# A hand-written order of the first eight steps, changed: conversions on GpSimd moved beside VectorE's rows, one product split around a weight folding, weight differences and sums moved, loads of x earlier

## The chip, the core and the metric

The kernel runs on one core of a Trainium2 chip. The metric is the device time of one execution in microseconds (us), from a median of several runs. The core has TensorE (PE, the matrix engine; PEld is its loading of weights), VectorE (DVE), ScalarE (ACT), GpSimd (POOL) and the queue of SyncE (SP), from which nearly all transfers (DMAs) are issued. Each engine works through its own list of instructions in order and waits for the others by semaphores. Matrix products write to PSUM, which here has eight banks; the rest lives in SBUF.

## The reference

An FFT over the sequence and one over the features, of which the real part is kept, and behind it a two-layer network with the quick Gelu:

```python
X = np.fft.fft(x, axis=1)          # x: (8, 3008, 256) float32
X = np.fft.fft(X, axis=2)
x = X.real.astype(np.float32).reshape(24064, 256)
h = x @ w_in                        # w_in: (256, 2048), 64-bit floats
g = h * (1.0 / (1.0 + np.exp(-1.702 * h)))
out = (g @ w_out).astype(np.float32)   # w_out: (2048, 256), 64-bit floats
```

## The kernel before, in words

**The two transforms.** The sequence of 3008 is taken as 47 times 64. For each of the eight batches `fold1` adds and subtracts mirrored rows and columns of x in SBUF (on GpSimd), `mix1` does the transform over 47 (TensorE), `spill` and `fill` turn the result through DRAM (`Td`), `rotate` corrects one column, `stage2` does the transform over 64, and `nyquist` spreads one special row. The transform over the 256 features is not done on x: `fold_w(n)` multiplies it into `w_in` once, chunk by chunk (n = 0 to 3, 512 columns each), and the result stands in `wcs[0]` (cosines) and `wcs[1]` (sines). Since x is real, rows k and -k of the hidden layer are sum and difference of the same two products.

**The weights.** `w_in` and `w_out` come as 64-bit floats and are made 32-bit on the chip, in eight chunks ("in" 0 to 3, "out" 0 to 3). For each chunk: `sizes` takes the absolute value of the upper word (L450 on ScalarE or L452 on VectorE), `clamp` bounds it (L456, GpSimd), `low` takes the lower word (L460, ScalarE), `high` shifts and masks (L486 and L487, VectorE), and `finish` adds both (L499 `finish_in`, L507 `finish_out`, GpSimd). `bounds(key)` calls sizes, clamp and low. `third` treats chunk "in" 2 in two halves of 512. `halved(n)` (L512, L513, VectorE) makes a sum and a difference of the finished chunk, which `fold_w(n)` (L533, copies L540 on ScalarE) multiplies; its copies of the result are needed by `hidden` and `first_row(n)`. `differences(n)` (L525, four subtractions on GpSimd) and `small_weights(n, lo, hi)` (L751, up to four sums on VectorE) prepare `w_out` for products in the manner of Strassen and Winograd: seven products for eight, and a second such level below.

**The steps.** The hidden layer is worked in 384 steps t: 8 batches, 3 blocks, 2 halves, 8 pairs of 128 columns each. The first eight (t = 0 to 7, the first group) run with plain products: `hidden(t)` makes the two sums pa and pb in two PSUM banks and copies pa to v (L584, ScalarE); `rows(t)` (VectorE: L614, two of L619, L621) makes both hidden rows; `activate(t)` (L625) is the Gelu; `product(t, lo, hi)` multiplies with `w_out` (a plan of eight entries; `lo` and `hi` cut it). `first_row(n)` (bank psf; copies L548 and L549) gives rows(2n), rows(2n + 1) and later steps a scale. From t = 8 on, a step is `begin` (x, in the bank `b0` or `b1`, on which ScalarE's `middle`, L634, has laid a start value), `forward` (L649), `doubled` (L646), `backward` (L653), `activate_back` (L656), `sums` (L664 and L665 on GpSimd; L671 and L672 on VectorE at odd t, in step t + 1), `deeper` (L695, L697, L699) and, three steps later, `product` with its `small_products` (L740).

**The order.** What each engine does next follows from the order in which the program is written out. For t < 8 that is `hidden(t)` and then the list `SCRIPT[t]`; at t = 7 `middle(8)` comes before `hidden(7)` and `begin(8)` right behind it. `extra` holds what is done at the end of a step t, entered by `at(t, ...)`; entries of one step run in the order in which they were entered. PLANS gives, for batch 0 and for the others, the steps of the sixteen folds, of the four `mix1`, the first `fill`, the `rotate`, the four loads of x for the batch after next (`load_x`, into the one buffer `xt`) and the three `stage2`. `paced(t)` issues a transfer of 4 bytes that waits for `forward(t)`, so that SP does not run ahead. Banks not named are taken in turn from `spare`; from step 5 on these are `o2`, `o3`, `o4` and `b2`: folding 3 takes o2 and o3, hidden(6) o4 (pa) and b2, first_row(3) o2, hidden(7) o3 (pa) and o4 (pb).

Of the kernel before, what the change touches and what calls it, by code (L numbers as in the profile page):

```python
# [121 lines left out]
def kernel(ctx: ExitStack, tc, x, w_in, w_out, tab1, tab2, out):  # L122
# [331 lines left out]
    def clamp(key, lo=0, n=1024):  # L454
        g = pre[key][0][:, lo:lo + n]
        nc.gpsimd.tensor_scalar(g, g, scalar1=TOP, scalar2=LOW, op0=ALU.min, op1=ALU.max)  # L456
# [5 lines left out]
    def third():  # L462

        prepare(in2)
        for h0 in (0, 512):
            sizes(in2, nc.vector, h0, 512)
            clamp(in2, h0, 512)
        low(in2)
        for h0 in (0, 512):
            high(in2, h0, 512)  # L470
            finish_in(2, h0, 512)

    def bounds(key):
        prepare(key)
        sizes(key, nc.scalar)
        clamp(key)
        low(key)

    def high(key, lo=0, n=1024):

        bits = pre[key][0][:, lo:lo + n].bitcast(U32)
        if lo == 0:
            made_a[key] = ring("a").bitcast(U32)
        a = made_a[key][:, lo:lo + n]
        dve = nc.vector
        dve.tensor_scalar(a, bits, scalar1=3, scalar2=0x3FFFFFF8, op0=ALU.logical_shift_left, op1=ALU.bitwise_and)  # L486
        dve.scalar_tensor_tensor(a, raw[key][:, lo:lo + n, 1], 0xC0000000, a, op0=ALU.bitwise_and, op1=ALU.bitwise_or)  # L487
# [5 lines left out]
    def finish_in(n, lo=0, k=1024):  # L493

        if lo == 0:
            wst[n] = op.tile([128, 2, 512], F32, tag="os", name="wst")
        key, part = ("in", n), slice(lo, lo + k)
        out = wst[n][:].rearrange("p i f -> p (i f)")[:, part]
        nc.gpsimd.tensor_tensor(out.bitcast(U32), made_a[key][:, part], pre[key][1][:, part], op=ALU.add)  # L499
# [158 lines left out]
    def sums(t, eng):  # L658

        if not NP <= t < len(steps):  # L660
            return
        n = width(t)
        if eng is nc.gpsimd:
            eng.tensor_tensor(right(t, S1, n), left(t, A21, n), right(t, A22, n), op=ALU.add)  # L664
            eng.tensor_tensor(left(t, S3, n), left(t, A11, n), left(t, A21, n), op=ALU.subtract)  # L665
            return
        if t % 2 == 0:
            return
        a11, s2 = (free(big[:], at_left(t - 1, q), [1024, 2], [1, n]) for q in (A11, S2))
        a12, s4, s1 = (free(big[:], at_right(t - 1, q), [1024, 2], [1, n]) for q in (A12, S4, S1))  # L670
        eng.tensor_tensor(s2, s1, a11, op=ALU.subtract)  # L671
        eng.tensor_tensor(s4, a12, s2, op=ALU.subtract)  # L672
# [69 lines left out]
    def small_weights(n, lo=0, hi=4):  # L742

        def y(i, at):
            return free(wot[:], (2 * n + i) * 4 * H + 2 * H + at, [NF // 2 * 4 * H, 2], [H, 2], [1, 64])

        b11, b12, b21, b22 = y(0, 0), y(0, 64), y(1, 0), y(1, 64)
        t1, t2, t3, t4 = (free(big[:], MADE + n * 1024 + q * 128, [512, 2], [64, 2], [1, 64]) for q in range(4))
        for out, i0, i1, how in ((t1, b12, b11, ALU.subtract), (t2, b22, t1, ALU.add), (t3, b22, b12, ALU.add),
                                 (t4, b21, t2, ALU.subtract))[lo:hi]:  # L750
            nc.vector.tensor_tensor(out, i0, i1, op=how)  # L751
# [218 lines left out]
    for h0 in (0, 512):  # L970
# [10 lines left out]
    halved(1)  # L981

    extra = {}
    PLANS = (((*range(9, 18), 22, 23, 24, 25, 26, 29, 30), (20, 28, 28, 36), 38, 43, (41, 42, 43, 44), (8, 20, 44)),
             ([g + k for g in (0, 8, 16, 24) for k in range(-2, 2)], (4, 20, 28, 28), 31, 35, (36, 38, 40, 42), (4, 20, 36)))

    def at(t, fn, *args):
        extra.setdefault(t, []).append((fn, args))
# [8 lines left out]
    if B > 1:  # L997
# [4 lines left out]
        at(6, nc.vector.memset, both_ends[0:1, 1, :], 0.0)  # L1002
        at(6, load_ends, 1)
        at(18, fold_ends, 1, nc.gpsimd)
    for i, t in enumerate((4, 5, 6, 7)):
        at(t, differences, i)
    for i, t in (1, 7), (2, 9):
        at(t, small_weights, i)
    for q, t in enumerate((11, 13, 14, 15)):
        at(t, small_weights, 3, q, q + 1)  # L1010
    for b in range(B):
        t0 = b * NBLK * NF
        if b + 2 < B:
# [24 lines left out]
        for blk in range(NBLK):  # L1038
# [7 lines left out]
    SCRIPT = (  # L1046
        [(nyquist, 0, 0), (fold_w, 1, ("o0", "o1")), (prepare, out0), (rows, 0, ((sizes, out0, nc.vector), (clamp, out0))), (high, out0)],
        [(low, out0), (finish, out0), (load_in, 3, nc.sync), (fill, 0, 4, NG), (activate, 0), (rows, 1)],
        [(first_row, 1), (activate, 1), (third,), (rows, 2), (halved, 2)],
        [(product, 0, 0, None), (product, 1, 0, None), (bounds, out1), (bounds, in3), (activate, 2), (high, out1), (finish, out1), (rows, 3),  # L1050
         (fold_w, 2), (activate, 3), (high, in3), (finish, in3)],
        [(first_row, 2), (rotate, 0, 4, NG, nc.scalar.copy), (rows, 4), (halved, 3)],
        [(product, 2, 0, None), (activate, 4), (bounds, out2), (rows, 5), (fold_w, 3), (activate, 5), (high, out2), (finish, out2)],
        [(first_row, 3), (product, 3, 0, None), (bounds, out3), (rows, 6), (activate, 6), (small_weights, 0), (high, out3), (finish, out3)],
        [(product, 4, 0, None), (rows, 7)])
    for t in range(n + LAG):
        if t < NP:
            if t == NP - 3:
                spare[:] = [tag for tag in spare if tag[0] == "o"] + ["b2"]
            if t == NP - 1:  # L1060
                middle(NP)
            hidden(t)
            if t == NP - 1:
                begin(NP)
                no_row(1024)
            for fn, *args in SCRIPT[t]:
                fn(*args)
            if t == NP - 1:
                doubled(NP)
                middle(NP + 1)  # L1070
        else:
            after, special = (any(fn in (mix1, stage2) for fn, _ in extra.get(k, ())) for k in (t - 1, t))
            assert t == NP or not special or (t - LAG) % NP == 1
            if t < n:
                begin(t, 1)
            if t == NP:
                activate(t - 1)
            if t < n:
                forward(t)
            if after:  # L1080
                swap(t - LAG - 3)
            opening = (t - LAG) % NP == 0 and t >= NP + LAG
            one, other = (1, 2, 4, 7), (5, 6, 3)
            cut = 0 if opening else 2
            if opening:
                small_products(t - LAG - 1, other[:2])
            else:
                product(t - LAG, 0, cut)
            if t + 1 < n:
                begin(t + 1)  # L1090
            if not after:
                small_products(t - LAG - 1, other[2 * opening:])
            if t > NP:
                spare[:] = ["l0", "l1", "l2", "b2"] if special else ["b2"]
                for fn, args in extra.get(t, ()):
                    if fn in (mix1, stage2):
                        fn(*args)
            product(t - LAG, cut, 6 if t - LAG == last else None)
            if after:
                small_products(t - LAG - 1, (7, *other, 1, 2, 4))  # L1100
            elif not special:
                small_products(t - LAG, one)
            if not special:
                swap(t - LAG - 2)
            if t < n:
                backward(t)
            if t + 1 < n:
                doubled(t + 1)
            if t < n:
                activate_back(t)  # L1110
                sums(t, nc.gpsimd)
            if t + 2 < n:
                middle(t + 2)
            for args in waiting:
                mixed(*args)
            waiting.clear()
            combine_small(t - LAG - 1)
            if t - LAG == last:
                product(last, 6, None)
            sums(t - 1, nc.vector)  # L1120
            turn_seconds()
            deeper(t - 2, 0)
            deeper(t - 3, 1)
        if t == NP:
            psu.close()
            low = ctx.enter_context(tc.tile_pool(name="low", bufs=1, space=PS))
            pot["low"] = low.tile([128, 3 * 512], F32, tag="low", name="low")
        if t >= LAG:
            combine(t - LAG)
            combine_last(t - LAG - 3)  # L1130
            turn_last(t - LAG - 4, 0)
            turn_last(t - LAG - 5, 1)
        if t == NP:
            spare[:] = ["l0", "l1", "l2", "b2"]
        for fn, args in extra.get(t, ()):
            if t <= NP or fn not in (mix1, stage2):
                fn(*args)
        if t == NP:
            turn_seconds()
# [28 lines left out]
```

## Time and profile before

| | |
|---|---|
| median of 3 runs | 1838.31 us (1837.73 to 1838.72) |
| the profiled execution | 1836.29 us, its span 1834.5 us |
| mean granted TensorE clock | 0.999 |
| busy share of the span | PE 99%, PEld 77%, DVE 81%, ACT 62%, POOL 54% |
| TensorE busy | 1819.8 us |
| DMA moved | 105.68 MB, mean 58 GB/s |
| steps 0 to 7 on TensorE | from 33.3 us to about 76.7 us of the span |

The profile is of one execution. Its parts and views give, for each engine, line of the kernel, operation and tile: when an instruction ran and how long (start, us), and after what wait ("idle before", with what ended it). In a view of waits, the columns are the line that waited, the line that ended the wait, the total, how often, and the longest. The same line number can serve many callers: L196 is the helper `halves`, through which most matmuls go, so the tile tells them apart (pa and pb: hidden; psf: first_row; psw: fold_w; o: product; x: begin). A matmul's end is modelled; the start of the next one says more.

### The profile page before, as it was taken

The page shows a single profiled execution, that of the slowest core. Times are in us where ns is not written, and L with a number is a line of the kernel's source. Part 1 is how long each engine was busy: PE and PEld are TensorE (multiplying, and loading weights), DVE is VectorE, ACT ScalarE, POOL GpSimd, SP SyncE. Part 2 cuts the span into 40 slices and gives each one's busy share as a digit, 9 for nine tenths or more (in the row PEclk, how much of TensorE's full clock was granted, in tenths as well). Part 3 has the DMA queues.
Part 4 walks back from the last instruction along what each step waited for, and adds up shares of the span by engine and source line. Part 5 has one row for each costly group of instructions (what it writes and reads, how often), then busy time and mean ns, then how long its engine had stood idle before and what let it go on. Part 6 is the DMA issues. An engine that isn't in the chain of part 4 may idle for free.

```text
span 1834.5 us, 55862 instructions
## 1 busy us (share of the span) xinstructions
PE 1819.8 (99%) x23656; PEld 1403.5 (77%) x23656; DVE 1481.7 (81%) x1927; ACT 1138.9 (62%) x2238; POOL 992.1 (54%) x1070
## 2 busy tenths in 40 slices
PE   8999999999999999999999999999999999999998
PEld 5677788777777777877778777787777877777775
DVE  7988878877888778887888878888788887878874
ACT  4556656666666656666665666666666666656663
POOL 3785556554656546565456644676446653444442
PEclk9999999999999999999999999999999999999999
DMA  9711151114210251212402124021331012100011
GB/s 283 185 53 35 43 115 28 47 36 101 54 53 23 52 117 21 62 36 67 89 22 59 32 67 86 22 64 27 87 66 39 14 27 64 30 19 14 18 24 24
DMA packets 151687, 105.68 MB, mean 58 GB/s; under 512 B 106212, under 2 KB 133094, under 8 KB 150878
## 3 DMA queue, kind: packets, MB, share of 16 engines
q1 hardware_dynamic: 148270, 99.09, 22.3%
q8 instruction: 186, 3.05, 0.7%
q10 hardware_dynamic: 3168, 3.03, 0.6%
q14 instruction: 63, 0.52, 0.1%
HBM read 64.81 MB, written 48.05 MB: 62 GB/s over the span
## 4 chain that ended last, share of the span: by engine, by line
PE 96%; DMA 2%; DVE 1%; issue 0%; POOL 0%; ACT 0%; SPq 0%; DVEq 0%; ACTq 0%; POOLq 0%
PE x L196 34%; PE o L196 27%; PE low L740 26%; PE o L740 4%; PE low L273 1%; PE low L393 1%; DMA xt<-in_x_dram 1%; PE po L196 0%; DMA big<-in_moe_w_in_dram 0%; DMA Td<-big 0%; DVE big L671 0%; DMA Td<-e 0%; DMA Tf<-big 0%; PE psw L533 0%; PE ps L393 0%
## 5 line engine op out<-in xcount | busy, mean ns | idle before, releaser
L664 POOL TENSOR_TENSOR big<-big 128x256 f32<-128x256 f32 (+1 forms) x376 | 366.4, 974 | 785.4 <-ACT big L656 764.5
L196 PE MATMUL x<-pq,wcs 128*64 128x256 f32 (+1 forms) x6016 | 767.7, 375 | 0.0
L196 PE MATMUL o<-big,wo 128*64 128x256 f32 (+1 forms) x4800 | 633.9, 376 | 1.0 <-DVE big L671 1.0
L196 PEld LDWEIGHTS x<-pq,wcs 128*64 128x64 f32 x6016 | 426.1, 137 | 170.9 <-issue 0.8
L196 PEld LDWEIGHTS o<-big,wo 128*64 128x64 f32 x4800 | 340.1, 137 | 144.9 <-issue 7.7
L646 ACT ACTIVATE g<-x 128x512 f32<-128x512 f32 (+1 forms) x376 | 221.7, 590 | 363.0 <-PE x L196 361.9
L665 POOL TENSOR_TENSOR big<-big 128x256 f32<-128x256 f32 (+1 forms) x376 | 381.3, 1014 | 0.0
L740 PE MATMUL low<-big 128*64 128x128 f32 (+1 forms) x5888 | 379.1, 270 | 0.0
L649 ACT ACTIVATE big<-x 128x512 f32<-128x512 f32 (+1 forms) x376 | 221.7, 589 | 233.9 <-PE x L196 207.7
L634 ACT ACTIVATE x<-nb,af 128x256 f32<-128x256 f32 (+1 forms) x752 | 352.7, 469 | 12.2
L653 DVE TENSOR_TENSOR big<-g,x 128x512 f32<-128x512 f32 (+1 forms) x376 | 250.5, 666 | 130.4 <-ACT big L649 129.9
L740 PEld LDWEIGHTS low<-big 128*64 128x64 f32 x5888 | 336.7, 137 | 24.9 <-DVE pq L403 0.2
L695 DVE TENSOR_TENSOR big<-big 128x1024 f32<-128x1024 f32 (+1 forms) x184 | 223.5, 1215 | 101.0 <-PE low L740 85.3
L656 ACT ACTIVATE big<-big 128x512 f32<-128x512 f32 (+1 forms) x376 | 231.6, 616 | 29.1 <-DVE big L653 28.0
L740 PE MATMUL low<-big,wo 128*64 128x128 f32 (+1 forms) x2944 | 221.8, 270 | 0.0
L699 DVE TENSOR_TENSOR big<-big 128x512 f32<-128x512 f32 (+1 forms) x184 | 191.7, 1042 | 0.0
L697 DVE TENSOR_TENSOR big<-big 128x512 f32<-128x512 f32 (+1 forms) x184 | 168.5, 916 | 16.6 <-PE o L196 0.9
L740 PEld LDWEIGHTS low<-big,wo 128*64 128x64 f32 x2944 | 174.0, 137 | 6.7 <-DVE big L699 0.5
L672 DVE TENSOR_TENSOR big<-big 128x512 f32<-128x512 f32 (+1 forms) x188 | 159.8, 850 | 6.5
L842 DVE TENSOR_TENSOR big<-big,low 128x512 f32<-128x512 f32 (+3 forms) x184 | 109.1, 610 | 35.1 <-PE low L740 31.6
L671 DVE TENSOR_TENSOR big<-big 128x512 f32<-128x512 f32 (+1 forms) x188 | 135.7, 722 | 0.9 <-POOL big L664 0.9
L740 PE MATMUL o<-big,wo 128*64 128x128 f32 (+1 forms) x1472 | 110.8, 270 | 0.0
(119 smaller groups left out, 1124.0 us busy)
## 6 DMA issues: line engine op xcount, KB each, us to landing
out_dram<-os SPq DMA_DIRECT2D x284, 64.0 KB
Td<-xt SPq DMA_DIRECT2D x56, 192.0 KB
t<-Td SPq DMA_DIRECT2D x21, 512.0 KB
xt<-in_x_dram SPq DMA_DIRECT2D x14, 512.0 KB
xt<-Xr SPq DMA_DIRECT2D x14, 512.0 KB
nb<-Nd SPq DMA_DIRECT2D x22, 256.0 KB
out_dram<-os SPq DMA_DIRECT2D x96, 56.0 KB
Xr<-in_x_dram SPq DMA_DIRECT2D x7, 752.0 KB
```

What stands on the lines that cost most here:

```text
L196: nc.tensor.matmul(out[c0:c0 + 64], lhsT=lhs[:, c0:c0 + 64], rhs=rhs, skip_group_check=True, **how)
L634: nc.scalar.activation(x[:, i * 256:i * 256 + n], nbt[b, blk][:, hh * 256:hh * 256 + n], ACTF.Copy, scale=af1[:, f:f + 1])
L646: nc.scalar.activation(two(g[:], n), two(xb[t][:], n), ACTF.Copy, scale=2.0)
L649: nc.scalar.activation(front(t), two(xb[t][:], width(t)), ACTF.Gelu_apprx_sigmoid)
L653: nc.vector.tensor_tensor(back(t), two(gt.pop(t)[:], n), two(xb.pop(t)[:], n), op=ALU.subtract)
L656: nc.scalar.activation(back(t), back(t), ACTF.Gelu_apprx_sigmoid)
L664: eng.tensor_tensor(right(t, S1, n), left(t, A21, n), right(t, A22, n), op=ALU.add)
L665: eng.tensor_tensor(left(t, S3, n), left(t, A11, n), left(t, A21, n), op=ALU.subtract)
L695: nc.vector.tensor_tensor(free(big[:], SUM, *both_), free(big[:], from11 + w, *twice), free(big[:], from11, [at_right(t, 0) + w - from11, ...
L697: nc.vector.tensor_tensor(s2, a11, s1, op=ALU.subtract)
L699: nc.vector.tensor_tensor(s4, a12, s2, op=ALU.subtract)
L740: nc.tensor.matmul(o, lhsT=lhs, rhs=rhs, start=first_in, stop=(p == NP - 2), skip_group_check=True)
```

## The change

Six things are moved; no arithmetic is changed.

1. In `third`, the second half of `finish_in(2)` is no longer called; step 2 calls it later, behind `bounds(out1)`, which moves from step 3 to step 2.
2. `bounds` can leave out its clamp. In step 3 the clamp of "in" 3 comes behind `finish(out1)`; `high` and `finish` of "in" 3 move from the end of step 3 to the end of step 4, behind `rows(4)`, and `halved(3)` from step 4 to step 5, behind `rows(5)`.
3. Product 3 moves from step 6 to step 5, half of its plan ahead of `fold_w(3)`, half behind it and `activate(5)`.
4. The four `differences` run at the ends of steps 5 to 8 and not 4 to 7. `small_weights(0)` moves from step 6 to the end of step 7, `small_weights(1)` from 7 to 8; the four parts of `small_weights(3)` run in steps 11, 13, 15 and 17, in the middle of the step behind GpSimd's `sums`, and not at the ends of 11, 13, 14 and 15.
5. Batch 1's folds: the first eight run one step later (10 to 17), the ninth at 21 and not 17; the other seven stay.
6. For batch 1, `fill` starts at step 37 and not 38 (`rotate` stays at 43), and the loads of x for batch 2 are issued at steps 39 to 42 and not 41 to 44.

```diff
--- before.py
+++ after.py
@@ -466,14 +466,15 @@
             sizes(in2, nc.vector, h0, 512)
             clamp(in2, h0, 512)
         low(in2)
-        for h0 in (0, 512):
-            high(in2, h0, 512)
-            finish_in(2, h0, 512)
-
-    def bounds(key):
+        high(in2, 0, 512)
+        finish_in(2, 0, 512)
+        high(in2, 512, 512)
+
+    def bounds(key, now=True):
         prepare(key)
         sizes(key, nc.scalar)
-        clamp(key)
+        if now:
+            clamp(key)
         low(key)
 
     def high(key, lo=0, n=1024):
@@ -981,7 +982,7 @@
     halved(1)
 
     extra = {}
-    PLANS = (((*range(9, 18), 22, 23, 24, 25, 26, 29, 30), (20, 28, 28, 36), 38, 43, (41, 42, 43, 44), (8, 20, 44)),
+    PLANS = (((*range(10, 18), 21, 22, 23, 24, 25, 26, 29, 30), (20, 28, 28, 36), 37, 43, (39, 40, 41, 42), (8, 20, 44)),
              ([g + k for g in (0, 8, 16, 24) for k in range(-2, 2)], (4, 20, 28, 28), 31, 35, (36, 38, 40, 42), (4, 20, 36)))
 
     def at(t, fn, *args):
@@ -1002,12 +1003,11 @@
         at(6, nc.vector.memset, both_ends[0:1, 1, :], 0.0)
         at(6, load_ends, 1)
         at(18, fold_ends, 1, nc.gpsimd)
-    for i, t in enumerate((4, 5, 6, 7)):
+    for i, t in enumerate((5, 6, 7, 8)):
         at(t, differences, i)
-    for i, t in (1, 7), (2, 9):
+    for i, t in (0, 7), (1, 8), (2, 9):
         at(t, small_weights, i)
-    for q, t in enumerate((11, 13, 14, 15)):
-        at(t, small_weights, 3, q, q + 1)
+    amid = {11 + 2 * q: (3, q, q + 1) for q in range(4)}
     for b in range(B):
         t0 = b * NBLK * NF
         if b + 2 < B:
@@ -1046,12 +1046,13 @@
     SCRIPT = (
         [(nyquist, 0, 0), (fold_w, 1, ("o0", "o1")), (prepare, out0), (rows, 0, ((sizes, out0, nc.vector), (clamp, out0))), (high, out0)],
         [(low, out0), (finish, out0), (load_in, 3, nc.sync), (fill, 0, 4, NG), (activate, 0), (rows, 1)],
-        [(first_row, 1), (activate, 1), (third,), (rows, 2), (halved, 2)],
-        [(product, 0, 0, None), (product, 1, 0, None), (bounds, out1), (bounds, in3), (activate, 2), (high, out1), (finish, out1), (rows, 3),
-         (fold_w, 2), (activate, 3), (high, in3), (finish, in3)],
-        [(first_row, 2), (rotate, 0, 4, NG, nc.scalar.copy), (rows, 4), (halved, 3)],
-        [(product, 2, 0, None), (activate, 4), (bounds, out2), (rows, 5), (fold_w, 3), (activate, 5), (high, out2), (finish, out2)],
-        [(first_row, 3), (product, 3, 0, None), (bounds, out3), (rows, 6), (activate, 6), (small_weights, 0), (high, out3), (finish, out3)],
+        [(first_row, 1), (activate, 1), (third,), (bounds, out1), (finish_in, 2, 512, 512), (rows, 2), (halved, 2)],
+        [(product, 0, 0, None), (product, 1, 0, None), (bounds, in3, False), (activate, 2), (high, out1), (finish, out1), (clamp, in3),
+         (rows, 3), (fold_w, 2), (activate, 3)],
+        [(first_row, 2), (rotate, 0, 4, NG, nc.scalar.copy), (rows, 4), (high, in3), (finish, in3)],
+        [(product, 2, 0, None), (activate, 4), (bounds, out2), (product, 3, 0, 4), (rows, 5), (halved, 3), (fold_w, 3), (activate, 5),
+         (product, 3, 4, None), (high, out2), (finish, out2)],
+        [(first_row, 3), (bounds, out3), (rows, 6), (activate, 6), (high, out3), (finish, out3)],
         [(product, 4, 0, None), (rows, 7)])
     for t in range(n + LAG):
         if t < NP:
@@ -1109,6 +1110,8 @@
             if t < n:
                 activate_back(t)
                 sums(t, nc.gpsimd)
+            if t in amid:
+                small_weights(*amid[t])
             if t + 2 < n:
                 middle(t + 2)
             for args in waiting:
```

## The prediction, made before the result was known

> **What bounds the kernel now.** I read the page's first part, then the waits of TensorE, then the order of time on TensorE and its neighbours in the first group. TensorE is busy almost throughout, at a granted clock of 0.999:
>
> ```profile
> PE 1819.8 (99%) x23656; PEld 1403.5 (77%) x23656; DVE 1481.7 (81%) x1927; ACT 1138.9 (62%) x2238; POOL 992.1 (54%) x1070
> ```
>
> So the change can only win what TensorE stands still. The waits of TensorE after the opening (line that waited, who ended it, total us, times, longest):
>
> ```profile
> PE o L196 <- DVE big L671: 1.0, 2, 0.8
> ...
> PE low L393 <- issue: 0.7, 1, 0.7
> ...
> PE psf L196 <- DVE big L621: 0.4, 1, 0.4
> PE psw L533 <- DVE big L512: 0.3, 1, 0.3
> PE psw L533 <- DVE big L513: 0.3, 1, 0.3
> ```
>
> These are too small, since a matmul's end is modelled. The order of time on TensorE (start, length) gives the rest:
>
> ```profile
> 50.78 1.04 PE L533 MATMUL psw<-big,small 128*64 128x512 f32 x2 [0.32 <-DVE big L512]
> 52.13 1.93 PE L533 MATMUL psw<-big,small 128*64 128x512 f32 x6 [0.31 <-DVE big L513]
> 53.88 1.08 PE L196 MATMUL pa<-pq,wcs 128*64 128x256 f32 x8
> ...
> 66.81 0.58 PE L196 MATMUL psf<-twos,wcs 128*64 128x1 f32 x16
> 67.24 3.65 PE L196 MATMUL o<-big,wo 128*64 128x256 f32 x32
> 70.72 1.03 PE L196 MATMUL pa<-pq,wcs 128*64 128x256 f32 x8
> 71.59 1.03 PE L196 MATMUL pb<-pq,wcs 128*64 128x256 f32 x8
> 72.45 0.93 PE L196 MATMUL x<-pq,wcs 128*64 128x226 f32 x8
> ```
>
> Starts that follow each other without a wait give TensorE's prices: a pa or pb 0.87, a product 3.47, first_row 0.44, the eight records of a folding 1.73 (35.92 to 37.64). The folding of chunk 2 should begin when the products end (43.35 + 6.94 = 50.29) and take 1.73, but step 4 starts at 53.88: 1.86 us stand still. For chunk 3, from 61.99 to 65.03, it is 1.31. ScalarE behind first_row(3), in the order of time:
>
> ```profile
> 67.56 1.21 ACT L450 ACTIVATE big<-big 128x1024 f32<-128x1024 f32 x1
> 68.64 1.20 ACT L460 ACTIVATE big<-big 128x1024 uint32<-128x1024 uint32 x1
> 69.71 1.09 ACT L625 ACTIVATE big<-big 128x1024 f32<-128x1024 f32 x1
> 70.67 0.95 ACT L634 ACTIVATE x<-nb,af 128x226 f32<-128x226 f32 x2
> ```
>
> The reader is to see that this row of four ends at 71.62, 4.37 us after first_row(3) ended (67.25), and that begin(8) (the x of 72.45) needs its last member; product 3 and hidden(7) cover it. VectorE against GpSimd, around 99 us:
>
> ```profile
> 99.17 2.70 DVE L671 TENSOR_TENSOR big<-big 128x452 f32<-128x452 f32 x1
> ```
> ```profile
> 98.85 1.27 POOL L247 TENSOR_TENSOR xt<-xt 111x510 f32<-111x510 f32 x1
> 100.09 0.67 POOL L664 TENSOR_TENSOR big<-big 128x226 f32<-128x226 f32 x1
> 100.71 0.66 POOL L665 TENSOR_TENSOR big<-big 128x226 f32<-128x226 f32 x1
> ```
>
> L671 takes 0.72 on average, and here it ends some 0.5 us after three GpSimd instructions in a row. VectorE's rows (L614 to L621, which read PSUM) keep 0.69, 0.86 and 0.69 beside L507 at 54 us. That is what "beside the rows" can use.
>
> **The change part by part.** All sums are against the profiled execution's 1836.29 us (span 1834.5 and 1.8 around it); the median of the runs shown is 1838.31, 2.0 above it.
>
> *Step 2 and the folding of chunk 2.* GpSimd gets the clamp of out1 (L456, 1.04) between the two halves of finish_in(2). The second half, 47.80 to 49.08 before, waits for VectorE's L487 (47.73) and then for the clamp: it ends near 49.9. It lies beside rows(2), which ends at 49.83. So halved(2) starts 0.2 later, but its second half no longer meets the clamp of in3 (L513 took 1.52 beside L456; alone 0.68), and ends at 51.2 and not 52.08. ScalarE's two conversions of out1 (1.1 each) now stand ahead of the copy v(3), which nobody needs before 53. Step 4 begins 1.75 after L513 (as 52.13 to 53.88): at 53.0, a gain of 0.88. Bounds: nothing (if the clamp gets ahead of L487) and 0.9.
>
> *Steps 3 to 5 and the folding of chunk 3.* high(in3), 1.9 us on VectorE, filled the time between rows(3) and rows(4). Now rows(4) follows rows(3) at once: that ends at 55.2, then activate(3) (1.06) and the copy v(4) (0.58) must pass on ScalarE before rows(4) can start at 56.9. VectorE idles 1.6. Then rows(4) 2.2, high(in3) 1.9 to 60.9, finish_in(3) on GpSimd (L499, 2.36) to 63.3 beside rows(5). halved(3) comes behind rows(5), and behind the clamp of out2, which is next on GpSimd and ready (1.04): its halves end near 64.9 and 65.5, not 62.09 and 63.23. TensorE, 0.84 earlier at hidden(5) (its first_row(2) still waits for rows(3)), does product 2 and half of product 3 by 62.9, waits, folds from 65.0 to 66.85, and covers ScalarE's copies with the other half: it stands still 2.24 where it was 1.31, a loss of 0.93. Bounds: a gain of 1.31 (halving in time) and a loss of 1.97 (one more GpSimd instruction of 1.04 in front).
>
> *Step 6.* Product 3 has left the place between first_row(3) and hidden(7). Behind first_row(3) ScalarE still owes the 4.37 us shown, and TensorE has only hidden(7), 1.73, to lay over it. So begin(8) starts 2.7 late; before, the cover was 5.2 and nothing was lost. Also pb(7) takes the bank of pa(6) (six banks in turn) and waits for rows(6), inside the same gap. Bounds: 2.6, and 3.2 if rows(6) holds activate(6) back. Product 4 starts 0.93 + 2.7 - 0.88 = 2.75 later than 73.22.
>
> *Differences and weight sums.* The differences (four of 0.8 to 0.95 on GpSimd) come a step later; the first products that need them run 30 us on. small_weights(0) and (1) move to the ends of steps 7 and 8 (3.4 us each beside GpSimd); VectorE then gives L653 of step 8 at about 82, as before. Differences(3) now stand between sums(8) and sums(9), so forward(10) comes near 93 instead of 88.95; begin(12), on a TensorE 2.75 late, wants its result near 96.4 and gets it: nothing, covered by 0.8 us; without that cover it costs what it is late. The last sums go into VectorE's pauses: at step 11 L695 waited 0.65 for ScalarE, and L751 (0.89) now fills that instead of standing before L671. L671 then ends 0.8 earlier, and the folding beside it is another half. TensorE stands from 100.92 to 101.92 and from 110.24 to 110.59 for it: a gain of 1.35; bounds 0 and 1.35.
>
> *Folds of x, fills, loads.* The folds go a step later, the ninth from 17 to 21; GpSimd waited 764 us for L656 over the run, and the groups that use them keep their steps: nothing. On SP the first fill now follows the last spill in the same step and waits for its landing; the store behind it was waiting for VectorE until 224.37 anyway. Loads 39 and 40 queue behind the stores that end at 231.8, so data starts near 232.6 instead of 234.0. rotate stays at 43, some 12 us after its last fill. TensorE's 0.68 of "issue" in stage2 at 249 falls where the DMA share is 1.0 (234 to 256); it would be 1.0 to about 254 still: I take nothing; bounds a gain and a loss of 0.7. The Trainium skill (DMA: Bandwidth & Descriptors, Queues, rings and completion order) says that an engine takes turns between queues packet by packet; by that the fetch is as slow as long as anything is queued, the same sum. No run here shows the packets.
>
> Sum: -0.88 + 0.93 + 2.7 - 1.35 = +1.4, so 1837.7 in the profile's terms and 1839.7 as a median. Bounds added: -0.9 - 1.3 + 2.6 - 1.35 - 0.7 = -1.65 and 0 + 1.97 + 3.2 + 0 + 0.7 = +5.9.
>
> **The rivals.** *Halving in time:* chunk 3's wait goes as its products are laid around it. For it: 1.73 of TensorE's work before and 1.73 behind. Against it: 1.6 us idle before rows(4) and the clamp. It gives 1.4 - 2.24 = -0.8: 1837.5.
>
> *VectorE locked out (the slower side).* In L671's 2.70 VectorE did not get in between GpSimd's instructions; in L512 against L525 (1.21 at 60.88) it did. If it does not where GpSimd is now queued tightly, L487 waits for the clamp of out1 (no 0.88), the sums bring no 1.35, and halved(3) waits once more (1.04): 1.4 + 3.3 = +4.7, 1843.0. It decides from 2.3 us on top of my sum. The Trainium skill (SBUF — State Buffer, Who interferes with whom) says that who issues first has the shared pair for one whole instruction; by it VectorE gets in after each, and the sum stays +1.4. The 2.70 beside three does not fit that, so I keep both.
>
> *The change does all it says:* ScalarE's chain is hidden too. Then 0.88 + 1.31 + 1.35 + 0.68 = 4.2 are won: 1834.1. Against it stand the 4.37 us over 1.73.
>
> **How the numbers follow.** 0.2% (3.7 us) is about what a measurement of this kernel can tell from no change. Forecast 0.47, halving in time 0.18, locked out 0.30, all it says 0.05. Faster is the last, 0.05; within 0.2% the first two, 0.65; slower the third, 0.30. The range leaves out the last case and the end of the bounds: 1836.6 (-1.7) to 1843.2 (+4.9); the forecast's own is 1838.1 to 1841.3.
>
> **What would show it.** Step 4's pa near 53.0; VectorE idle before L614 of step 4; psw of chunk 3 not before 64.5; in step 7 an x whose wait is ended by ScalarE L634, near 75; no wait for L671 at 100 to 115; the "issue" wait of L393 still there. I am wrong if begin(8) follows hidden(7) without a gap, or if psw of chunk 3 runs on without one; and the sum is too small if new waits of TensorE appear past step 16.

## The result, and the profile after

The changed kernel takes 1844.08 us (median of 10, 1840.38 to 1845.96), the kernel before 1837.99 in the same series: a ratio of 1.0030, 95% interval [1.0022, 1.0039]. It is 0.3% slower, 6 us. A second series, below, gives 1.0024 [1.0014, 1.0034]. The forecast was 1839.7, with a range up to 1843.2.

The profiled execution's span is 1843.2 us, 8.7 more than before. Five stretches of TensorE's time, each from the start of one group of matmuls to the start of another, say where they lie; "again" is the changed kernel's second profile.

| stretch | before | after | again | forecast |
|---|---|---|---|---|
| start to hidden(1) | 37.64 | 41.50 | 41.10 | 0 |
| hidden(1) to product 4 | 35.58 | 40.36 | 40.37 | +2.75 |
| product 4 to begin(16) | 37.80 | 36.78 | 36.79 | -1.35 |
| begin(16) to the end of step 44's stage2 | 139.32 | 140.68 | 140.51 | 0 |
| from there to the end | 1584.16 | 1583.88 | 1583.73 | 0 |

The first stretch holds no instruction that the change touches. Over the 14 profiles of this study it took 37.5 to 41.5 us, long and short with either order, so its +3.9 is left out of what follows. TensorE's order of time after, with the lines that answer to those shown of before (behind the changed `bounds`, line numbers are one higher in the changed kernel and those made from it: L512 is now L513, L533 is L534, L634 is L635):

```profile
54.56 2.44 PE L534 MATMUL psw<-big,small 128*64 128x512 f32 x8 [0.24 <-DVE big L513]
56.82 1.08 PE L196 MATMUL pa<-pq,wcs 128*64 128x256 f32 x8
...
68.86 3.18 PE L534 MATMUL psw<-big,small 128*64 128x512 f32 x7 [2.02 <-DVE big L513]
...
78.90 1.08 PE L196 MATMUL pb<-pq,wcs 128*64 128x256 f32 x8 [1.12 <-DVE big L622]
81.04 0.98 PE L196 MATMUL x<-pq,wcs 128*64 128x226 f32 x8 [1.06 <-ACT x L635]
81.86 3.62 PE L196 MATMUL o<-big,wo 128*64 128x256 f32 x32
```

Counted from hidden(1), step 4's pa comes at 15.32 and not 16.24. The folding of chunk 3 (68.86) waits 2.02 for halved(3), and pb(7) and begin(8) wait for rows(6) and for ScalarE's L635. All three are where the forecast put them. The waits of TensorE add one that grew, L393 for issue:

```profile
PE psw L534 <- DVE big L513: 2.3, 2, 2.0
PE low L393 <- issue: 2.2, 1, 2.2
```

What the forecast didn't have is in the table of windows around that folding (after the length: busy time of PE, PEld, DVE, ACT and POOL; then the granted clock, the DMA share and GB/s):

```profile
66.00:68.00 2.00, 0.84 (x8) 0.34 (x4) 1.51 (x3) 0.04 (x1) 2.00 (x2) 1.00 1.07 381
68.00:70.00 2.00, 1.14 (x4) 0.47 (x6) 1.97 (x4) 0.00 (x0) 0.17 (x1) 0.89 0.96 292
70.00:72.00 2.00, 2.00 (x8) 1.19 (x6) 1.18 (x1) 0.58 (x1) 0.67 (x1) 0.50 0.27 61
72.00:74.00 2.00, 2.00 (x16) 1.80 (x14) 0.00 (x0) 1.07 (x2) 2.00 (x3) 0.76 0.98 249
```

Behind the standstill the clock is at 0.50. The means 0.89 and 0.76 place its beginning at 69.56 and its end at 72.96 (0.11 and 0.24 of 2 us, over the half that is missing): 3.4 us at half speed, 1.7 lost.

### The profile page after: what moved, and what is told of

Read it like the earlier page. It is cut to its first block, busy times and chain, and to the rows that moved or that the text cites. A ratio compares the mean times of both kernels' runs of the same rounds, so it can differ in the third digit from the quotient of the medians.

```text
span 1843.2 us, 55864 instructions
## 1 busy us (share of the span) xinstructions
PE 1822.2 (99%) x23656; PEld 1403.0 (76%) x23656; DVE 1479.5 (80%) x1927; ACT 1138.5 (62%) x2238; POOL 992.2 (54%) x1070
## 4 chain that ended last, share of the span: by engine, by line
PE 95%; DVE 2%; DMA 1%; POOL 1%; ACT 1%; issue 0%; DVEq 0%; POOLq 0%; ACTq 0%
PE x L196 34%; PE o L196 27%; PE low L741 25%; PE o L741 4%; PE low L273 1%; PE low L393 1%; DMA big<-in_moe_w_in_dram 1%; DMA xt<-in_x_dram 1%; PE po L196 0%; PE psw L534 0%; POOL wst L500 0%; DVE big L488 0%; PE ps L393 0%; PE pa L196 0%; POOL xt L906 0%
## 5 line engine op out<-in xcount | busy, mean ns | idle before, releaser
L635 ACT ACTIVATE x<-nb,af 128x256 f32<-128x256 f32 (+1 forms) x752 | 352.7, 469 | 12.2
L673 DVE TENSOR_TENSOR big<-big 128x512 f32<-128x512 f32 (+1 forms) x188 | 161.0, 857 | 6.5
L672 DVE TENSOR_TENSOR big<-big 128x512 f32<-128x512 f32 (+1 forms) x188 | 131.6, 700 | 0.9 <-POOL big L665 0.9
```

The costliest lines, as they stand in the source:

```text
L635: nc.scalar.activation(x[:, i * 256:i * 256 + n], nbt[b, blk][:, hh * 256:hh * 256 + n], ACTF.Copy, scale=af1[:, f:f + 1])
```

## The experiments

The theory after the result: the schedule of the forecast is right, and on top come a halved clock behind the new standstill and a slower fetch of instructions with the denser loads (the profile calls that wait only "issue"; that it is the fetch is inferred). The rivals: VectorE is locked out by GpSimd, or the slow matmuls come of the interleaving of the folding with product 3. Times are judged by their interval, the stretches by the profiles.

**a1_filled.** Two matmuls into a free bank where TensorE stood still:

```diff
-(product, 3, 0, 4), (rows, 5), (halved, 3), (fold_w, 3),
+(product, 3, 0, 4), (warm, 2, "b2"), (rows, 5), (halved, 3), (fold_w, 3),
```

> The changed kernel with two idle matmuls (1.9 us, result unused, into the bank b2) between the first half of product 3 and the folding of chunk 3, where TensorE stood still for 2.2 us. Theory 1 (a standstill of some 2 us is followed by a halved granted clock for some 3.4 us): the clock stays at 1.00 between 60 and 85 us of the span, hidden(1) to product 4 takes 38.4 and not 40.36 us, and the time falls by about 2. Theory 2 (the slow matmuls behind the folding come of the interleaving with product 3 or of contention, not of the standstill): 40.4 or more stays, and the clock drops as before.

hidden(1) to product 4 took 38.72 at a clock of 1.00; the time ratio is 1.0024 [1.0015, 1.0034]. Taken alone it looks like theory 1. But the next kernel, whose standstill is not filled, took 38.68 at 1.00 as well. So a standstill of 2 us does not always halve the clock, and this run alone decides nothing. Its clock does fall elsewhere: behind L393's wait of 2.31 us for issue it is at 0.50 from 253.8 to 257.2 us.

**a2_loads_back.** `37, 43, (39, 40, 41, 42)` is again `38, 43, (41, 42, 43, 44)` in PLANS.

> The changed kernel with the fills from step 38 and the loads of x at steps 41 to 44, as before. If the loads, issued closer together, made the fetch of instructions in stage2 slower, the issue wait of L393 falls from 2.2 to 0.7 us and the stretch from begin(16) to the end of that stage2 from 140.7 to 139.3. If that wait is chance or belongs to the phase of the program, it stays between 1.5 and 2.5.

L393 waited 1.08, the stretch was 139.60, the ratio 1.0016 [1.0006, 1.0025]. Its two waits are those of the changed kernel:

```profile
64.87 2.01 PE L534 MATMUL psw<-big,small 128*64 128x512 f32 x7 [2.01 <-DVE big L513]
...
75.37 0.98 PE L196 MATMUL x<-pq,wcs 128*64 128x226 f32 x8 [1.07 <-ACT x L635]
```

So without a halved clock the schedule costs 38.68 - 35.58 = 3.1, and the halved clock 40.36 - 38.68 = 1.7, the half of 3.4. Why the clock fell behind one standstill of 2.0 us and not behind this one is taken up in the last section.

**b1_sums_only.** The kernel before with parts 4 and 5 of the change (differences, weight sums, folds).

> The kernel before with the differences, weight sums and folds of the change alone (script and loads as before). If the sums in VectorE's pauses do what the prediction took, the wait for L671 goes and product 4 to begin(16) takes 36.5 to 36.8 and not 37.8 us. If VectorE is locked out as in the 2.70 us before, 37.8 stays.

Product 4 to begin(16) took 36.76, as expected. hidden(1) to product 4 fell too, to 34.72, which was not expected. The ratio is 0.9990 [0.9980, 0.9999]. VectorE's order of time shows why: halved(3) no longer shares its time with the differences (1.21 and 1.22 before).

```profile
63.76 0.69 DVE L512 TENSOR_TENSOR big<-wst 128x512 f32<-128x512 f32 x1 [0.43 <-POOL wst L499]
64.36 0.68 DVE L513 TENSOR_TENSOR big<-wst 128x512 f32<-128x512 f32 x1
```

**b2_step2_only.** The kernel before with `finish_in(2, 512, 512)` and `bounds(out1)` in step 2, the clamp of chunk 3 not put off.

> The kernel before with only the conversion of out1 moved into step 2 (its clamp between the halves of finish_in(2)). The prediction's step: the folding of chunk 2 ends 0.9 earlier, hidden(1) to product 4 34.7 and not 35.6 us. The rival (VectorE locked out by the clamp): 35.6 or more.

35.53, no gain; ratio 1.0000 [0.9991, 1.0010]. The clamp of chunk 3 is now the next on GpSimd behind finish_in(2) and meets the first half of halved(2): L512 took 1.51 and TensorE waited 1.10 for it. In the change the same move gains 0.92, as there that clamp stands behind finish(out1). The gain belongs to both edits together; the clamp of out1 locked nothing out (L487 took 1.65, 1.66 before).

**c1_loads_only.** The kernel before with the PLANS entry of the change for fills and loads.

> The kernel before with only the fills from step 37 and the loads of x at steps 39 to 42, as in the change. Theory: the closer loads make the fetch in stage2 slower, so L393 waits 2.0 to 2.5 us for issue, begin(16) to the end of that stage2 takes 140.6 to 141.2 and the time rises by 1 to 1.5. Rival (the wait is chance of the phase): the wait is 0.7 to 1.5 as in the four profiles with the old loads, the stretch 139.3 to 140.0, the time unchanged.

L393 waited 2.29, the stretch was 141.33, the ratio 1.0009 [1.0001, 1.0018]. Of the 2.0 us by which the stretch grew, 1.6 are the wait. The rest is a halved clock, from 252.4 to 255.8 us, in which the matmuls behind the wait are slow (1.03 at full clock):

```profile
254.63 1.62 PE L196 MATMUL x<-pq,wcs 128*64 128x256 f32 x8
```

Over all profiles the wait is 0.68 to 1.63 with the old loads (seven, mean 1.2) and 1.23 to 2.31 with the new (six, mean 2.0). The ranges overlap, but on average the wait is 0.8 longer with the denser loads.

**c2_loads_earliest.** All three fills at step 37, loads at steps 37, 37, 38, 38.

> The kernel before with all three fills at step 37 and the loads of x right behind them at steps 37 and 38. If the wait for issue comes of transfers that are under way during stage2, they are now over before it: no wait for issue in L393, 138.6 from begin(16) to the end of that stage2, about 1 us faster than before. If it comes of many transfers queued at once, whenever they end, a wait of 2 us or more stays or appears elsewhere.

L393 no longer waits, yet the stretch is 139.40 and the ratio 1.0012 [1.0002, 1.0022], slower. The wait moved. The transfers of 4 bytes that pace SP queue behind the loads, and `forward` four steps on may not overwrite what they read:

```profile
ACT big L649 <- DMA Tk<-big: 4.1, 1, 4.1
DVE big L653 <- ACT big L649: 4.0, 1, 4.0
...
PE x L196 <- ACT g L646: 0.8, 1, 0.8
```

That 0.8 takes back the 0.7 of before; what else its time holds, the profile (span 1836.2) doesn't show. The mean granted clock of its twelve executions is 0.9980 (0.9987 for the kernel before).

**a3_product_back.** The changed kernel with product 3 whole in step 6, behind first_row(3).

> The changed kernel with product 3 whole in step 6, behind first_row(3), as before. By the prediction's schedule the standstill at the folding of chunk 3 grows from 2.2 to 3.9 us and the gap ahead of begin(8) goes: hidden(1) to product 4 takes 37.9 us (38.7 with the split, without a halved clock), 1.7 more if the clock halves behind the longer standstill. If the gap ahead of begin(8) does not come of the missing product, it stays, and the stretch takes 40 or more.

The gap ahead of begin(8) is gone, so it came of the missing product. TensorE waited 3.72 at the folding and then ran at half clock:

```profile
68.03 3.85 PE L534 MATMUL psw<-big,small 128*64 128x512 f32 x8 [3.72 <-DVE big L513]
```
```profile
68.00:70.00 2.00, 1.97 (x7) 0.84 (x8) 1.97 (x3) 0.00 (x0) 0.00 (x0) 0.73 0.68 172
70.00:72.00 2.00, 2.00 (x8) 1.03 (x7) 0.35 (x1) 0.67 (x2) 1.50 (x2) 0.50 0.70 179
72.00:74.00 2.00, 2.00 (x29) 1.63 (x25) 0.01 (x1) 1.94 (x3) 1.92 (x3) 0.92 1.09 179
```

The three means (0.73, 0.50, 0.92) make 3.4 us at half speed again. hidden(1) to product 4 took 39.28, of which 1.7 are the clock's. No product is interleaved with this folding, so the interleaving is not what slows it. Ratio 1.0023 [1.0013, 1.0033].

**a4_back_filled.** The same with `(warm, 4, "b2")` ahead of `(rows, 5)`.

> The kernel of a3_product_back with four idle matmuls (3.8 us, results unused) in the standstill of 3.7 us ahead of the folding of chunk 3; everything else as there. If the halved clock seen behind that standstill (0.50 for some 3 us) comes of the standstill, the clock now stays at 1.00 there and hidden(1) to product 4 takes 37.8 to 38.1 and not 39.28 us, though TensorE does more. If the halving comes of something else (the folding itself, the transfers), it is seen again and the stretch is 39 or more.

37.83, at a clock of 1.00, with more work on TensorE:

```profile
63.07 3.70 PE L363 MATMUL warm<-wcs 128*128 128x512 f32 x8
66.79 2.53 PE L534 MATMUL psw<-big,small 128*64 128x512 f32 x8
```
```profile
66.00:68.00 2.00, 1.98 (x7) 0.64 (x7) 1.97 (x4) 0.00 (x0) 0.20 (x1) 1.00 1.04 343
68.00:70.00 2.00, 2.00 (x14) 0.64 (x10) 1.21 (x1) 1.22 (x3) 0.65 (x1) 1.00 0.47 110
```

The ratio is 1.0011 [1.0002, 1.0020], and the mean granted clock of its ten executions is 0.9987, of the eight of a3_product_back 0.9978, of 90 of the kernel before 0.9987. So in these two profiles the halving comes with the standstill and goes with it. The ratios differ by 0.0012, about 2 us, but their intervals overlap.

**b4_split_only.** The kernel before with product 3 split around the folding, all else as it was.

> The kernel before with product 3 split around the folding of chunk 3, all conversions where they were. By the prediction's schedule the folding no longer waits (a gain of 1.3) but begin(8) is exposed by 2.7: hidden(1) to product 4 takes 36.9 and not 35.6 us. If the split only hides the folding, 34.3.

36.83, as the schedule said; ratio 1.0013 [1.0005, 1.0022]. The folding has no wait left and begin(8) has two:

```profile
65.77 1.92 PE L533 MATMUL psw<-big,small 128*64 128x512 f32 x8
...
73.58 1.08 PE L196 MATMUL pb<-pq,wcs 128*64 128x256 f32 x8 [1.12 <-DVE big L621]
75.72 0.98 PE L196 MATMUL x<-pq,wcs 128*64 128x226 f32 x8 [1.06 <-ACT x L634]
```

**a5_high_first.** a2_loads_back with chunk 3 converted as before:

```diff
-(rows, 3), (fold_w, 2), (activate, 3)],
-[(first_row, 2), ..., (rows, 4), (high, in3), (finish, in3)],
+(rows, 3), (fold_w, 2), (activate, 3), (high, in3), (finish, in3)],
+[(first_row, 2), ..., (rows, 4), (halved, 3)],
```

> The changed kernel with the old loads, and with high and finish of chunk 3 ahead of rows(4) and halved(3) ahead of rows(5), as before; product 3 stays split. If high(in3) behind rows(4) made the standstill at the folding (the prediction's step), TensorE no longer waits there, the gap ahead of begin(8) stays at some 2.2 us, and hidden(1) to product 4 takes 36.1 us (38.7 with high behind rows(4)). If the clamp of out2 or another GpSimd instruction made it, 38 or more.

36.69. The folding follows without a wait:

```profile
64.47 1.92 PE L534 MATMUL psw<-big,small 128*64 128x512 f32 x8
...
74.43 1.77 PE L196 MATMUL x<-pq,wcs 128*64 128x226 f32 x8 [1.06 <-ACT x L635]
```

So high(in3) behind rows(4), with halved(3) behind rows(5), made that standstill; how much of it was the clamp of out2, which this edit takes out of the way too, isn't separated. A halved clock is in the stretch again (0.9 of it), here behind the waits of pb(7) and begin(8): these eight matmuls take 1.77 and not 0.98, and the granted clock is 0.53 from 74 to 76 us and 0.62 from 76 to 78. Ratio 1.0005 [0.9996, 1.0014].

**e1_kept_parts.** Parts 4 and 5, the conversion of out1 in step 2 and the late clamp of chunk 3; the rest as before.

> The change without the three parts that cost time: the conversion of chunk 3 and product 3 as in the kernel before, fills and loads as before; kept are the conversion of out1 in step 2 with the clamp of chunk 3 behind finish(out1), and the differences, weight sums and folds. By the sum: hidden(1) to product 4 33.9 to 34.2 (35.58 before), product 4 to begin(16) 36.8 (37.8 before), in all 2.4 us faster than the kernel before, a ratio near 0.9987. If the gains of the parts are not to be added, 0.5 to 1.5 us.

1836.04 us against 1838.25: a ratio of 0.9986 [0.9977, 0.9994], faster than the kernel before by 2.2 us, near the sum's 2.4. The two stretches show only 1.5 of it: 36.78 in the second as expected, 35.13 in the first and not 34. With its clamp late, high of chunk 3 is late too, and the folding waits 0.81; the moves of step 2 gain nothing over b1_sums_only here.

**f1_change_again.** The changed kernel, a second series.

> The changed kernel once more, to see whether the parts add up. Sum of the parts so far: +3.1 to product 4 without a halved clock, -1.0 to begin(16), +0.8 to +1.5 in stage2, +0.6 for the lower mean clock, in all 3.5 to 4.2 us, a ratio of 1.0019 to 1.0023; in the profile hidden(1) to product 4 is 38.7, or 40.4 with a halved clock, and hidden(1) starts between 37.5 and 41.5. If something is missing from the sum, the ratio is 1.003 again, and a stretch of the trace shows it.

1.0024 [1.0014, 1.0034], with a halved clock at the same folding (40.37) and 2.00 us for L393. Its sum of 3.5 to 4.2 us lies within the interval (2.6 to 6.2 us); in the first series (4.0 to 7.2) only its upper end does. Of that series' 6.1 us, 1.9 to 2.6 are not accounted for.

## Why the prediction was wrong

- **Bound and method: right.** TensorE's order decides. What moved is in the three stretches that the forecast named or priced.
- **Step 2: right.** 0.88 forecast, 0.92 measured. That the late clamp belongs to it was not said; b2_step2_only shows it.
- **Steps 3 to 5: right in mechanism and in place.** L615 of rows(4) waited 1.60 for v(4) (forecast 1.6), L513 took 1.52 beside the clamp of out2, and the folding started 27.36 after hidden(1) (forecast 65.0 - 37.64 = 27.36; that it agrees to the hundredth is luck, since 65.0 was a rounded estimate). a5_high_first removes the standstill.
- **Step 6: right.** a3_product_back and b4_split_only show both sides; in b4_split_only the two gaps, ahead of pb(7) and begin(8), make 2.6 (forecast 2.7). The schedule as a whole cost 3.1 without a halved clock, where the forecast had 2.75. The difference lies behind the folding: from its start to product 4, a2_loads_back takes 11.31 and b4_split_only, with the same matmuls, 10.77. Why is open; in a2_loads_back the records of the folding, product 3 and hidden(6) interleave.
- **The step that failed first: "waits, folds from 65.0 to 66.85".** It priced the standstill at its own length. The clock of the matmuls behind it was taken as 1.00, as the profile before shows it past the opening. It fell to 0.50 for 3.4 us in both profiles of the changed kernel: 1.7 more. Not every execution need have it: the mean clock of the changed kernel's 19 was 0.9984 and of the kernel before 0.9987 (90), and 0.0003 of 1838 us are 0.6. That difference is about one standard error, so the average price is not clear of noise.
- **The step that failed second: "I take nothing; bounds a gain and a loss of 0.7".** The wait for issue rose by 0.8 on average and by 1.5 in the profile, beyond the bound. I had argued that transfers are under way at that time in either case; c1_loads_only shows that it matters how they are queued. The Trainium skill's turn-taking packet by packet (DMA: Bandwidth & Descriptors, Queues, rings and completion order) was read as the same wait for any backlog, and the measurements differ.
- **The sums in the pauses: right, mis-sized.** 1.35 forecast, 1.02 measured. The wait for L671 (now L672) went, but VectorE's lock-out moved to L673 (2.35, as L672 1.03 before) and to the next weight sum, in step 13, and a new wait of 0.35 stands ahead of begin(16):

```profile
106.99 0.62 DVE L672 TENSOR_TENSOR big<-big 128x452 f32<-128x452 f32 x1
107.64 2.35 DVE L673 TENSOR_TENSOR big<-big 128x452 f32<-128x452 f32 x1
...
111.46 2.48 DVE L752 TENSOR_TENSOR big<-wo,big 128x256 f32<-128x256 f32 x1
```

- **"Differences: nothing": wrong in the kernel before,** where moving them freed halved(3) (0.9 in b1_sums_only). In the change the clamp of out2 took their place.
- **The rivals.** The time came out on the side of the slower rival, but not by its mechanism: the clamp of out1 did not hold L487 up, and the gain in step 2 was had. "Halving in time" and "all it says" did not happen.

Sum by what the runs showed: +3.1 - 1.0 + 0.8 + 0.6 = +3.5 us on average; in the profile, +3.1 + 1.7 - 1.0 + 1.4 - 0.3 = +4.9, and +3.9 of the opening. The first series measured +6.1 and the second +4.8; the rest stays open.

## What to carry to other kernels

Where the matrix engine is the bound, an instruction that is moved forward to fill one gap leaves another open where it stood: ask which chain on the other engines it covered there, and add up that chain. Price a standstill by its length and by what the engine's clock may do behind it, and fill one that can't be avoided. A batch of changes should be taken apart: here e1_kept_parts, the parts that win, is 2 us faster than the kernel before, and the moves around chunk 3 and product 3 and the denser loads cost more than that.

## What the runs showed of the hardware

- A standstill of 2.0 us (after, again) or 3.7 us (a3_product_back) was followed by 3.4 us at a granted clock of 0.50; another of 2.0 us (a2_loads_back) was not; where that of 3.7 us was filled with idle matmuls, the clock stayed at 1.00. L393's waits of 2.31 (a1_filled) and 2.29 us (c1_loads_only) were followed by 3.4 us at half clock too, with no folding near. The Trainium skill (TensorE: Matmul & The Clock Gate, Part 1: The HAM clock gate) speaks of windows of about 3.4 us and of half rate after an idle one; the length agrees, but 2.0 us of standing still were enough here.
- The drops lie on a fixed period. In the profile after, the half-speed time around 37 us (windows' means 0.86, 0.50, 0.79) begins at 35.43, the one at 69.56 is 34.13 later, ten times 3.413, and the last drop of the execution, at 1841.08, a further 1771.52, 519 times 3.4133. "Again" and a3_product_back have 34.13 between their first two as well, and a5_high_first 40.96, twelve times 3.413.
- The period would explain why a2_loads_back kept its clock. Counted back from its last drop (1834.89), one period ends at 63.37, within its standstill (62.86 to 64.87), so that 1.50 us of it lie in the next; the standstill after (66.84 to 68.86) lies whole between 66.15 and 69.56. By the same count the place that a1_filled fills lies whole in one period (62.65 to 66.06), and there the clock stayed at 1.00. From hidden(1) on, in all 14 profiles, the waits of TensorE that the profile lists come to 1.86 us or more in six periods, each followed by a drop, and to 1.79 or less in the others, none followed by one until the matmuls end. No run moved a standstill against the period on purpose, so this is read from traces and not tested. Ahead of hidden(1) the sums do not separate so: in the profile after, 1.25 us had a drop behind them and 1.89 had none.
- TensorE's wait for issue in a burst of 64 small matmuls was 0.68 to 2.31 us while the DMA share was near 1.0, and none when the transfers had ended before it.
- VectorE's lock-out by several GpSimd instructions in a row (2.70 before, 2.35 and 2.48 after) shows in whichever instruction stands at that place.
